# First loads of a transformer block: which queue issues them, in what order, and the last 64 weight rows by two transfers

## The chip, the cores and the metric

The kernel runs on one core of one Trainium2 chip. The metric is the device time of one execution in microseconds (us): the median of three runs is 211.99 us (211.5 to 212.01). A core has TensorE (PE in the profile; PEld is its weight loads), VectorE (DVE), ScalarE (ACT), GpSimd (POOL) and SyncE (SP). SP computes nothing here; its program is a list of DMA issues. ACT can issue DMAs too, between its own instructions. All DMAs of the core run on the same 16 DMA engines.

## The reference

```python
S, D, H, Dh, F, W = 2048, 448, 16, 28, 1792, 256
xn = layernorm(x)                                   # x: [1, 2048, 448], bf16
q, k, v = split(xn @ wqkv)                          # wqkv: [448, 3 * 448], 16 heads of 28
p = softmax(where(0 <= i - j < W, q k^T / sqrt(Dh), -1e9))
out = x + (p v) @ wo + (gelu(xn @ w_gate) * (xn @ w_up)) @ w_down
```

One layer normalisation feeds two branches that are added to x: attention in a sliding window of 256 keys, and a gated feed-forward layer.

## The kernel before

The 2048 rows of x are 16 tiles of 128 rows (tile t is `x_sb[:, t, :]`), in four blocks of 512 rows, numbered 0 to 3. For each block the kernel makes q and k transposed (`qT`, `kT`), four groups of four heads each, and v (`v_sb`), then scores, Exp on ACT, masks, the product with v, and the feed-forward layer; work of the next block, and the feed-forward products of this one, are woven in by lists (`plan`) that set the order by hand. Each engine runs its own list in order. A row that waits holds up all that is behind it on its engine.

The contraction length 448 is cut in 128 + 128 + 128 + 64 rows. The weight rows 0 to 383 are the dense part. The last 64 rows are held twice, on partitions 0 to 63 and 64 to 127, so that two products over 64 rows can run in the two halves of the PE array. Three tiles in SBUF take the weights of the first stage:

- `wraw` ([128, 4, 896]): the columns of q and k, raw. Its plane 3 takes the last 64 rows: q's columns on partitions 0 to 63, k's on 64 to 127.
- `wv` ([128, 4, 448]): the columns of v. Its plane 3 takes the last 64 rows of v twice.
- `wqp`, `wkp`, `w3p`: q's and k's weights with each head's 28 columns padded to 32. Engines copy them out of `wraw`: L754 a group or two of dense rows, L792 the last 64 rows for all groups (`w3p`).

The steps that the prediction follows, by line and in the order in which the program has them:

- L85 to L98: the first loads. x's tile 0 and tiles 2 and 3 are issued by SP, tile 1 by ACT (L87). ACT then issues the dense rows of q's and k's first 112 columns, that is of group 0 (L90). SP goes on with v's dense rows (L91), the last 64 rows in four transfers of 64 partitions (L93 twice, L95 twice), x's tiles 4 to 7 (L96), and the other 336 columns of q and of k (L98 twice), all on one queue.
- L152: nine products on zeroed data ahead of everything, and a tenth a little later.
- L157 to L200, for tiles 0 to 3: statistics (DVE), 1/sigma (ACT), normalisation (L176 on DVE, tile 1 L184 on ACT), four transposes on PE (L199), and a copy into `xnT` (L200).
- L204: v of tile 0 and then of tile 1, dense rows (`pv<-wv,xnT`), q and then k of group 0, dense rows (`s<-xnT,wqp` and `s<-xnT,wkp`).
- L210: the last 64 rows: q and k of group 0 with `w3p`, then v of tiles 0 to 3 with plane 3 of `wv`. L204 again: v of tile 3, and of tile 2 a little later.
- L257 and L258: the copies of q (ACT) and k (DVE) out of PSUM. L240: the copies of v. On DVE stand, right behind the first k copy, the L754 copies of group 1 (from the L98 loads), the copy of v's tile 3, the L754 copies of groups 2 and 3, and the copy of v's tile 2.
- L688 and L693: scores and Exp of group 0; L204 and L210: q and k of groups 1, 2 and 3.
- L505: the first feed-forward products (`ue<-xnT,wu`). They take a pair of the four PSUM banks b0 to b3, and the pair is free once q and k of group 2 have been copied out.

Every DMA that SP or ACT issues gets one of eight semaphores, DMAHW0 to DMAHW7, in turn. The transfer that takes a semaphore for the second time waits until the first one has landed. So SP can run at most eight transfers ahead, and a late one holds up the ninth behind it.

The few lines that a sentence can't say (before):

```python
    for c in (0, D):
        nc.scalar.dma_start(out=wraw[:, 0:3, c:c + 4 * Dh], in_=wqk[:, :, c:c + 4 * Dh])                 # L90
    nc.sync.dma_start(out=wv[:, 0:3, :], in_=rows(A_wqkv, 0, 3)[:, :, 2 * D:3 * D])                      # L91
    for a in range(2):
        nc.sync.dma_start(out=wraw[64 * a:64 * a + 64, 3, 0:D], in_=A_wqkv[384:448, a * D:(a + 1) * D])  # L93
...
    qk_halves(0, 0, pq, pk)                                  # PE: L210, needs w3p
    for t in range(4):
        v_half(t, pvs[t], t < 2)                             # PE: L210, needs wv[:, 3, :]
    qk_copies(0, 0, pq, pk)                                  # ACT L257, DVE L258
    pads(nc.vector.tensor_copy, wqp, slice(1, 2))            # DVE: L754, needs the L98 loads
    v_copy(0, pvs[0], nc.scalar.copy)
    v_copy(1, pvs[1], nc.scalar.copy)
    pads(nc.vector.tensor_copy, wkp, slice(1, 2))            # DVE: L754
    v_dense(3, pvs[3], False)
    v_copy(3, pvs[3], nc.vector.tensor_copy)                 # DVE: L240
```

Of the kernel before, what the change touches and what calls it, by code (L numbers as in the profile page):

```python
# [16 lines left out]
S, D, H, Dh, F = 2048, 448, 16, 28, 1792  # L17
# [10 lines left out]
def kernel(  # L28
# [11 lines left out]
    nc = tc.nc  # L40
# [23 lines left out]
    wv = const.tile([P, 4, D], bf16, name="wv")  # L64
    v_sb = const.tile([P, NT, H, 32], bf16, name="v_sb")
    wraw = blk.tile([P, 4, 2 * D], bf16, name="wraw", tag="hT")
# [5 lines left out]
    def rows(w, c0, n):  # L72
        return w[c0 * P:(c0 + n) * P, :].rearrange("(c p) n -> p c n", p=P)
# [10 lines left out]
    wqk = rows(A_wqkv, 0, 3)[:, :, 0:2 * D]  # L84
    nc.sync.dma_start(out=x_sb[:, 0, :], in_=xv[:, 0, :])  # L85
    nc.vector.memset(x_sb[:, 1, 0:1], 0.0)
    nc.scalar.dma_start(out=x_sb[:, 1, :], in_=xv[:, 1, :])  # L87
    nc.sync.dma_start(out=x_sb[:, 2:4, :], in_=xv[:, 2:4, :])
    for c in (0, D):
        nc.scalar.dma_start(out=wraw[:, 0:3, c:c + 4 * Dh], in_=wqk[:, :, c:c + 4 * Dh])  # L90
    nc.sync.dma_start(out=wv[:, 0:3, :], in_=rows(A_wqkv, 0, 3)[:, :, 2 * D:3 * D])  # L91
    for a in range(2):
        nc.sync.dma_start(out=wraw[64 * a:64 * a + 64, 3, 0:D], in_=A_wqkv[384:448, a * D:(a + 1) * D])  # L93
    for a in range(2):
        nc.sync.dma_start(out=wv[64 * a:64 * a + 64, 3, :], in_=A_wqkv[384:448, 2 * D:3 * D])  # L95
    nc.sync.dma_start(out=x_sb[:, 4:8, :], in_=xv[:, 4:8, :])  # L96
    for c in (0, D):
        nc.sync.dma_start(out=wraw[:, 0:3, c + 4 * Dh:c + D], in_=wqk[:, :, c + 4 * Dh:c + D])  # L98
    load_ffn(wu, B_w_up, slice(0, 3))
# [981 lines left out]
```

## Time and profile before

| what | value |
|---|---|
| time, median of three runs | 211.99 us (211.5 to 212.01) |
| span of the profiled execution, first to last instruction | 210.4 us |
| what the median has beyond the span (start and finish) | 1.6 us |
| PE busy | 205.3 us, 98% of the span |
| DVE, ACT, POOL busy | 156.6, 134.5, 44.3 us |
| DMA traffic | 15.68 MB in 24890 packets |

The profiled execution's own time is its span of 210.4 us and what lies around it; the times shown are those of the three runs. Starts in the profile are us from the first instruction. A row of the timeline has start, length, engine, line, operation, tile written <- tiles read, and how many instructions are merged in it; in brackets stands the idle time ahead of it and what ended it. PE's ends are modelled, so the starts of its rows are what to go by. SPq and ACTq rows are the issue of a DMA, not its transfer. A packet is one piece that one DMA engine moves, here a row of a tile.

### The profile page before, as it was taken

To read this page: it belongs to the slowest core of one execution; us is meant where nothing else is said; L and a number is where in the kernel's file an instruction comes from. 1 tells how busy PE (TensorE), PEld (TensorE's weight loads), DVE (VectorE), ACT (ScalarE), POOL (GpSimd) and SP (SyncE) were. 2 spreads that over 40 slices of the span, in tenths; PEclk is the share of its full clock that TensorE was granted. 3 is DMA by queue.
4 is the path that set the end of the run, shared out by engine and by line. 5 is a ranking of instruction groups with operands and counts; after the bars stand their busy time and mean duration, and the time that the engine had idled before them with its cause. 6 is when DMAs were issued, how large, how long until landed. Compare 5 with 4: busy or idle time off the path is not lost. (4 is left out here: it accounts for less than half of the span.)

```text
span 210.4 us, 6677 instructions
## 1 busy us (share of the span) xinstructions
PE 205.3 (98%) x2842; PEld 98.4 (47%) x2842; DVE 156.6 (74%) x360; ACT 134.5 (64%) x132; POOL 44.3 (21%) x89
## 2 busy tenths in 40 slices
PE   7899999999999999999999999999999999999994
PEld 2443444544454545444445444544444454544572
DVE  6798989899788985696438897395385699596532
ACT  4689896956677977413778788523587787756000
POOL 5289932241000220040000112013000022032000
PEclk9999999999999999999999999999999999999999
DMA  5999599973341001003331000100000010100011
GB/s 171 277 244 207 112 207 224 296 237 82 74 103 53 25 11 31 9 3 72 71 75 47 25 3 24 23 3 21 22 5 0 3 47 3 45 9 16 3 47 50
DMA packets 24890, 15.68 MB, mean 75 GB/s; under 512 B 9208, under 2 KB 24728, under 8 KB 24856
## 3 DMA queue, kind: packets, MB, share of 16 engines
q1 hardware_dynamic: 23912, 14.93, 30.2%
q8 instruction: 23, 0.38, 0.7%
q10 hardware_dynamic: 944, 0.29, 0.6%
q14 instruction: 11, 0.09, 0.2%
HBM read 9.26 MB, written 2.41 MB: 55 GB/s over the span
## 5 line engine op out<-in xcount | busy, mean ns | idle before, releaser
L693 ACT ACTIVATE p_sb<-sc 128x2048 bf16<-128x2048 f32 x38 | 71.4, 1879 | 16.9 <-PE sc L688 11.7
L545 ACT ACTIVATE p_sb<-gt 128x1024 bf16<-128x1024 f32 x28 | 28.6, 1025 | 31.3 <-PE gt L505 30.4
L628 POOL TENSOR_TENSOR oN<-oc,l 128x512 bf16<-128x512 f32 x16 | 20.7, 1298 | 120.5 <-DVE l L641 120.5
L505 PE MATMUL gt<-xnT,wg 64*128 64x512 bf16 x224 | 45.6, 376 | 0.0
L414 PE MATMUL po<-wd,hT 128*128 128x448 bf16 (+1 forms) x224 | 44.7, 347 | 0.0
L505 PE MATMUL gt<-xsw,wg 64*128 64x512 bf16 x168 | 40.7, 376 | 0.0
L613 DVE TENSOR_TENSOR p_sb<-p_sb,masks 128x256 bf16<-128x256 bf16 (+1 forms) x98 | 30.9, 369 | 7.4 <-ACT p_sb L693 7.4
L555 DVE TENSOR_TENSOR hT<-p_sb,u 128x512 bf16<-128x512 bf16 x34 | 21.8, 675 | 13.5 <-PE u L505 13.5
L414 PEld LDWEIGHTS <-hT 128*128 128x128 bf16 x238 | 21.9, 98 | 19.1 <-issue 2.2
L505 PEld LDWEIGHTS <-wg 64*128 64x128 bf16 x392 | 19.0, 94 | 22.3
L505 PEld LDWEIGHTS <-wu 64*128 64x128 bf16 x392 | 18.7, 94 | 22.2 <-issue 0.4
L505 PE MATMUL u<-xnT,wu 64*128 64x512 bf16 x136 | 28.1, 376 | 0.0
L505 PE MATMUL u<-xsw,wu 64*128 64x512 bf16 x102 | 24.7, 376 | 0.0
L505 PE MATMUL ue<-xnT,wu 64*128 64x512 bf16 x88 | 18.0, 377 | 0.0
L647 DVE TENSOR_TENSOR oc<-oc,ov 128x512 f32<-128x512 f32 (+1 forms) x16 | 10.4, 656 | 10.0 <-ACT oc L645 9.9
L505 PE MATMUL ue<-xsw,wu 64*128 64x512 bf16 x66 | 16.3, 377 | 0.0
L688 PE MATMUL sc<-qT,kT 28*64 28x320 bf16 (+4 forms) x736 | 16.2, 259 | 0.0
L402 DVE TENSOR_TENSOR res<-po,x_sb 128x448 bf16<-128x448 f32 (+1 forms) x14 | 8.1, 605 | 7.8 <-PE po L414 6.7
L688 PEld LDWEIGHTS <-kT 28*64 28x64 bf16 x736 | 8.1, 103 | 12.3 <-issue 11.0
L522 DVE CAST hT<-ue 128x512 bf16<-128x512 f32 x16 | 10.5, 685 | 2.7 <-PE ue L505 2.7
L645 ACT COPY oc<-ov 128x512 f32<-128x512 f32 x16 | 9.3, 585 | 4.0 <-PE ov L662 4.0
L641 DVE STREAM_TRANSPOSE l<-inv_all 128x512 f32<-128x512 f32 x16 | 11.1, 701 | 0.1
(115 smaller groups left out, 257.0 us busy)
## 6 DMA issues: line engine op xcount, KB each, us to landing
out_dram<-res SPq DMA_DIRECT2D x15, 112.0 KB
wd<-in_B_w_down_dram SPq DMA_DIRECT2D x2, 784.0 KB
x_sb<-in_A_x_dram SPq DMA_DIRECT2D x3, 448.0 KB
xsw<-xnT SPq DMA_DIRECT2D x6, 192.0 KB
wg<-in_B_w_gate_dram SPq DMA_DIRECT2D x2, 560.0 KB
wu<-in_B_w_up_dram SPq DMA_DIRECT2D x4, 224.0 KB
wu<-in_B_w_up_dram SPq DMA_DIRECT2D x2, 336.0 KB
wraw<-in_A_wqkv_dram SPq DMA_DIRECT2D x2, 252.0 KB
```

Source lines behind the costliest of these rows:

```text
L414: nc.tensor.matmul(po[:, 0:w], lhsT=x[:, k, tt * P:(tt + 1) * P], rhs=wt[:, k, lo:up], start=start and n == 0, stop=stop and n == len(term ...
L505: nc.tensor.matmul(ps, lhsT=w[64 * hi:64 * hi + 64, c, p * P:(p + 1) * P], rhs=xchunk(qb, hi, c, qb * QB, QB), start=c == 0, stop=c == 6, ...
L522: copy(out=hTs[qb][:, p + 7 * i, :], in_=us[i])
L545: nc.scalar.activation(out=ges[p][:, :, :], in_=gt[:, :, :], func=ACT.Gelu_apprx_tanh)
L555: nc.vector.tensor_tensor(out=hT[:, p + 7 * i, :], in0=ge[:, i, :], in1=u, op=ALU.mult)
L613: nc.vector.tensor_tensor(out=reg, in0=reg, in1=m, op=ALU.mult)
L628: nc.gpsimd.tensor_tensor(out=oN[:, g, :], in0=oc[:, :], in1=inv, op=ALU.mult)
L641: nc.vector.transpose(out=l1[:, :, :], in_=inv_all[:, 4 * qb + g, :].unsqueeze(2).to_broadcast([P, 16, 32]))
L645: nc.scalar.copy(out=oc[:, :], in_=ov[0][:, :])
L647: nc.vector.tensor_tensor(out=oc[:, q0:], in0=oc[:, q0:], in1=ov[1][:, q0:], op=ALU.add)
L688: nc.tensor.matmul(ss[k0:k0 + nk, j, col:col + nq], lhsT=kT[r, g, kt * P + k0:kt * P + k0 + nk], rhs=qT[r, g, ring(qb).start + q0:ring(qb) ...
L693: nc.scalar.activation(out=p_sb[:, :, 0:ncol], in_=ss[:, :, 0:ncol], func=ACT.Exp, scale=SCALE)
```

## The change

The first q and k columns move from ACT's queue to SP's, behind v's dense rows. x's tiles 4 to 7 move ahead of the last 64 rows. These rows come by two transfers in place of four: each writes all 128 partitions of plane 3 and reads a source of shape [2, 64, 448]. For q and k the source's first step goes from q's columns to k's; for v it has a step of zero, so the same 64 rows are read twice. Nothing else differs; lines behind the change have numbers smaller by two.

```diff
     nc.sync.dma_start(out=x_sb[:, 2:4, :], in_=xv[:, 2:4, :])
+    nc.sync.dma_start(out=wv[:, 0:3, :], in_=rows(A_wqkv, 0, 3)[:, :, 2 * D:3 * D])
     for c in (0, D):
-        nc.scalar.dma_start(out=wraw[:, 0:3, c:c + 4 * Dh], in_=wqk[:, :, c:c + 4 * Dh])
-    nc.sync.dma_start(out=wv[:, 0:3, :], in_=rows(A_wqkv, 0, 3)[:, :, 2 * D:3 * D])
-    for a in range(2):
-        nc.sync.dma_start(out=wraw[64 * a:64 * a + 64, 3, 0:D], in_=A_wqkv[384:448, a * D:(a + 1) * D])
-    for a in range(2):
-        nc.sync.dma_start(out=wv[64 * a:64 * a + 64, 3, :], in_=A_wqkv[384:448, 2 * D:3 * D])
+        nc.sync.dma_start(out=wraw[:, 0:3, c:c + 4 * Dh], in_=wqk[:, :, c:c + 4 * Dh])
     nc.sync.dma_start(out=x_sb[:, 4:8, :], in_=xv[:, 4:8, :])
+    nc.sync.dma_start(out=wraw[:, 3, 0:D], in_=A_wqkv[384:448, 0:2 * D].rearrange("p (a n) -> a p n", a=2))
+    nc.sync.dma_start(out=wv[:, 3, :], in_=A_wqkv[384:448, 2 * D:3 * D].unsqueeze(0).to_broadcast([2, 64, D]))
     for c in (0, D):
         nc.sync.dma_start(out=wraw[:, 0:3, c + 4 * Dh:c + D], in_=wqk[:, :, c + 4 * Dh:c + D])
```

SP's list from its first DMA, before; a row has the line, the tile written and the tensor read, the shape written, and the semaphores that the row waits for.

```order
L85 DMA x_sb<-in_A_x_dram 128x448
L88 DMA x_sb<-in_A_x_dram 128x2x448
L91 DMA wv<-in_A_wqkv_dram 128x3x448
L93 DMA wraw<-in_A_wqkv_dram 64x448 x2
L95 DMA wv<-in_A_wqkv_dram 64x448 [waits DMAHW0_49]
L95 DMA wv<-in_A_wqkv_dram 64x448 [waits DMAHW1_49]
L96 DMA x_sb<-in_A_x_dram 128x4x448 [waits DMAHW2_49]
L98 DMA wraw<-in_A_wqkv_dram 128x3x336 [waits DMAHW3_49]
L98 DMA wraw<-in_A_wqkv_dram 128x3x336 [waits DMAHW4_49]
```

The same stretch of SP's list with the change.

```order
L85 DMA x_sb<-in_A_x_dram 128x448
L88 DMA x_sb<-in_A_x_dram 128x2x448
L89 DMA wv<-in_A_wqkv_dram 128x3x448
L91 DMA wraw<-in_A_wqkv_dram 128x3x112 x2
L92 DMA x_sb<-in_A_x_dram 128x4x448
L93 DMA wraw<-in_A_wqkv_dram 128x1x448
L94 DMA wv<-in_A_wqkv_dram 128x1x448 [waits DMAHW0_49]
L96 DMA wraw<-in_A_wqkv_dram 128x3x336 [waits DMAHW1_49]
L96 DMA wraw<-in_A_wqkv_dram 128x3x336 [waits DMAHW2_49]
```

The last 64 rows (L93 and L95 before, L93 and L94 now) stand behind x's tiles 4 to 7 instead of ahead of them. The two loads of the other q and k columns waited for ACT's two q and k transfers (DMAHW3 and DMAHW4); now they wait for x's tiles 1 to 3 (DMAHW1 and DMAHW2).

ACT's list from its first DMA to the first normalisation, before.

```order
L87 DMA x_sb<-in_A_x_dram 128x448 [waits DVE_49]
L90 DMA wraw<-in_A_wqkv_dram 128x3x112 x2
L137 ACT_TABLE_LOAD
L166 ACTIVATE lnv<-mv_all,eps_t 128x1 [waits DVE_49]
L167 ACTIVATE rstd_all<-lnv 128x1 [waits Activation_49]
```

The same stretch with the change.

```order
L87 DMA x_sb<-in_A_x_dram 128x448 [waits DVE_49]
L135 ACT_TABLE_LOAD
L164 ACTIVATE lnv<-mv_all,eps_t 128x1 [waits DVE_49]
L165 ACTIVATE rstd_all<-lnv 128x1 [waits Activation_49]
L164 ACTIVATE lnv<-mv_all,eps_t 128x1 [waits DVE_49]
```

The two issues are gone from ACT; the rest of its list is as it was. The lists of PE, DVE and POOL hold the same rows in the same order.

## Prediction

> **What bounds the kernel now.** I read the page first, then the waits, then busy time by stage, then the timeline of the first 20 us engine by engine, last the DMA packets. Of the page, the span, PE's share, and PE and DMA over the span in 40 slices:
>
> ```profile
> span 210.4 us, 6677 instructions
> PE 205.3 (98%) x2842; PEld 98.4 (47%) x2842; DVE 156.6 (74%) x360; ACT 134.5 (64%) x132; POOL 44.3 (21%) x89
> ...
> PE   7899999999999999999999999999999999999994
> ...
> DMA  5999599973341001003331000100000010100011
> ```
>
> PE runs from end to end; DMA is full only in the first fifth. The waits of PE, over the whole span:
>
> ```profile
> PE wps L152 <- DVE wo L126: 1.4, 1, 1.4
> PE pv L204 <- DMA wv<-in_A_wqkv_dram: 0.6, 1, 0.6
> ```
>
> Only the second can be touched: 0.6 us for v's weights. Busy time by stage (PE, PEld, DVE, ACT, POOL, granted clock, DMA share, GB/s):
>
> ```profile
> 0.00:2.00 2.00, 0.57 (x2) 0.28 (x3) 0.99 (x8) 0.00 (x0) 1.32 (x7) 1.00 0.05 10
> 2.00:4.00 2.00, 2.00 (x7) 0.64 (x5) 1.06 (x4) 1.46 (x2) 1.66 (x2) 1.00 0.89 258
> ...
> 12.00:14.00 2.00, 2.00 (x25) 0.80 (x9) 2.00 (x5) 1.96 (x2) 1.73 (x7) 1.00 1.13 224
> 14.00:20.00 6.00, 6.00 (x79) 2.33 (x86) 5.81 (x15) 5.64 (x8) 5.45 (x18) 1.00 1.20 244
> 20.00:30.00 10.00, 10.00 (x222) 4.78 (x224) 8.35 (x18) 8.94 (x10) 7.67 (x27) 1.00 0.77 137
> ```
>
> From 12 to 20 us PE, DVE and ACT are all full, and so are the DMA engines. A delay that gets into the first 20 us has nowhere to be absorbed, and after that PE has no wait in which to catch up: it reaches the end. So the question is when the first loads land.
>
> The starts on PE:
>
> ```profile
> 7.34 0.73 PE L204 MATMUL pv<-wv,xnT 128*128 128x448 bf16 x3 [0.65 <-DMA wv<-in_A_wqkv_dram]
> ...
> 9.04 0.82 PE L204 MATMUL s<-xnT,wqp 128*128 128x512 bf16 x3
> ...
> 10.44 0.39 PE L210 MATMUL s<-xnT,w3p 64*128 64x512 bf16 x2
> 10.66 0.54 PE L210 MATMUL pv<-wv,xnT 64*128 64x448 bf16 x4
> ...
> 18.52 0.38 PE L505 MATMUL ue<-xnT,wu 64*128 64x512 bf16 x1
> ```
>
> And on DVE: a wait for x's tile 0, then what needs late weights:
>
> ```profile
> 2.94 0.63 DVE L157 BATCH_NORM_STATS2 st<-x_sb 128x6 f32<-128x448 bf16 x1 [0.91 <-DMA x_sb<-in_A_x_dram]
> ...
> 8.55 0.42 DVE L200 COPY xnT<-tp 128x512 bf16<-128x512 bf16 x1 [0.86 <-PE tp L199]
> ...
> 8.89 0.27 DVE L792 COPY w3p<-wraw 128x448 bf16<-128x448 bf16 x1
> ...
> 11.69 0.26 DVE L754 COPY wkp<-wraw 128x336 bf16<-128x336 bf16 x1
> ...
> 17.45 0.68 DVE L258 CAST kT<-pk 128x512 bf16<-128x512 f32 x1
> ```
>
> **The prices.** DMA queues (q1 is SP's, q10 ACT's) in three windows: packets, MB, share of 16 engines. First 4 to 8 us, then 8 to 10 us, then 81 to 86 us, this one with its share in 40 slices of 0.125 us:
>
> ```profile
> q1 hardware_dynamic: 1223, 1.00, 84.8%
> q10 hardware_dynamic: 591, 0.13, 15.1%
> ```
>
> ```profile
> q1 hardware_dynamic: 840, 0.56, 102.6%
> ```
>
> ```profile
> DMA  0016100101011212131222202212221210000000
> ...
> q1 hardware_dynamic: 144, 0.11, 13.9%
> k<-kT SPq DMA_DIRECT2D x4, 12.0 KB
> k<-qT SPq DMA_DIRECT2D x3, 16.0 KB
> ```
>
> A row of 896 B: 0.848 x 16 x 4 us / 1223 = 44 ns on its engine. A row of 224 B: 0.151 x 64 us / 591 = 16 ns. A row of 672 B (most of the second window): 1.026 x 32 us / 840 = 39 ns. The third window holds seven transfers whose outermost dimension is 4, in flight together. They are given 0.139 x 80 = 11.1 us of engine time within slices 9 to 33, that is 3.1 us: 3.6 engines at work on average, where the 128-row loads of the first microseconds keep all 16 busy. A transfer with an outermost 4 seems to run on four engines.
>
> **The change, part by part.** *v's rows ahead of the q and k columns.* In front of v's rows now stand only x's tiles 0 to 3; the two column loads (768 rows of 224 B, 48 per engine, 0.8 us) no longer share the engines with them. They land up to 0.8 us earlier, and the wait of 0.65 us at 7.34 goes. Next late is the copy of tile 3's transposes (8.55), which moves with PE; q of group 0 starts near 8.5 instead of 9.04: 0.5 us ahead. The q and k columns are behind v now, but by the same count they end no later than before.
>
> *ACT without its two issues, SP with them.* DVE's first statistics and ACT's first use of them, then SP's waits:
>
> ```profile
> 3.60 0.18 DVE L158 BATCH_NORM_AGGREGATE mv_all<-st 128x2 f32<-128x6 f32 x1
> ...
> 3.82 0.29 ACT L166 ACTIVATE lnv<-mv_all,eps_t 128x1 f32<-128x1 f32 x1
> ```
>
> ```profile
> SPq L98 <- DMA wraw<-in_A_wqkv_dram: 1.7, 2, 1.3
> ```
>
> For ACT it is nothing: its first work waits for DVE's statistics, which end at 3.8. SP gets two issues and drops two. x's tiles 4 to 7 and the loads behind them go out earlier, since fewer issues stand ahead of them and L98 no longer waits 1.7 us for ACT's transfers. PE had no other wait for a load, so this is worth nothing to it, but it keeps the DMA queues full.
>
> *The last 64 rows in two transfers.* This is the term that decides. Each writes 128 partitions from a source whose outermost dimension is 2. No transfer of before pairs 128 with 2. One bound is all 16 engines, 8 rows each, 0.35 us a transfer. The other, going on from the outermost 4 above, is two engines, 64 rows each, 64 x 44 = 2.8 us. I take two engines: the row with the outermost 4 is the nearest, and a split over the outermost dimension that both sides share allows no more.
>
> [...]
>
> When do they land? An engine has in front of them 88 rows of x and v (11 x 128 rows over 16 engines) and 48 short rows: 88 x 44 + 48 x 16 ns = 4.7 us. It starts at 1.9 (5% of the first 2 us). So on the two engines q's and k's rows move from 6.6 to 9.4 and v's to 12.2, and only then their share of the other q and k columns (24 rows of 39 ns a load, 0.94 us each): 13.1 and 14.1. What lands is seen later than counted: tile 0 counts 1.9 + 8 x 0.044 = 2.25 and DVE starts at 2.94, 0.7 later. With 0 to 0.7 us added, k's columns are usable between 14.1 and 14.8; I take 14.5, and for v's rows 12.6.
>
> PE stands before v's last rows at 10.1 (10.66 less the 0.5 gained) and waits until 12.6: 1.9 us behind before. DVE stands before the L754 copy of k's columns, at 11.69 before, and goes on at 14.5: 2.8 us behind, with v's copies, two statistics, four normalisations and the k copies queued behind it. DVE makes up 0.2 (idle in 14 to 20 us). The k copy of group 2 frees the PSUM banks for the first `ue` products; it ends at 18.13 and they start at 18.52, a margin of 0.4. So `ue` starts 2.8 - 0.2 - 0.4 = 2.2 us late, and PE's own 1.9 is inside that. `w3p`, about 1.2 us late, is hidden behind the wait for v's rows.
>
> **The sum.** The gain of 0.5 is swallowed by the later wait; +2.2 us remain. On the span: 210.4 + 2.2 = 212.6. The median lies 1.6 above the span and the change doesn't touch what lies there, so 211.99 + 2.2 = 214.2. This case reaches from 213.2 (rows of 41 ns and no lag: k's columns at 13.5, 1.8 - 0.6 = 1.2 us) to 215.3. That end comes from v's dense rows before: 1.9 + 56 x 0.044 + 0.8 = 5.2 counted, 7.34 seen; if 1.5 of these 2.1 us come on top of 14.1, DVE goes on at 15.6, 3.9 - 0.6 = 3.3 us late.
>
> **Rivals.** *Spread over all engines.* If the two transfers use 16 engines, each takes 0.35 us, they land at about 7.3 plus the lag, ahead of PE's need at 9.9, and what stays is the gain: 0.5 us, 211.5. For it: the written side has 128 partitions, as the fast loads have. Against it: the outermost-4 rows. It decides if both have landed by 10.1, that is if a transfer takes less than (10.1 - 6.6 - 0.7) / 2 = 1.4 us. [...]
>
> *Two engines, but the delay is covered.* Rows of 35 ns and no lag put k's columns at 13.0: 1.3 - 0.6 = 0.7 us, and about 0.1 less if DVE uses what it has free in 20 to 30 us (8.35 of 10): 212.6. Against it: 44 ns is the mean of a full queue, and these two engines stay full.
>
> *The backlog reaches the next block.* Two engines carry 2 x 56 extra rows, 4.9 us, and a transfer has landed only when its slowest engine is done; everything until 20 us is full, and 20 to 30 us has 2.3 us free. The swap of the next block's rows and its first use:
>
> ```profile
> 22.79 2.31 SPq L486 DMA_DIRECT2D xsw<-xnT  x2
> ```
>
> ```profile
> 29.78 0.73 PE L339 MATMUL pv<-wvs,xsw 64*128 64x448 bf16 x6
> ```
>
> From the end of the issue to the use are 4.7 us, and PE is 2.2 late itself; if landing takes over 2 us there, the swap is what PE waits for, and the shift is between 2.6 and 4.9: about 3.5, 215.5.
>
> **Chances.** Two engines with a stall of about 2.2 us: 0.60. Spread, with the gain: 0.20. Backlog in the next block: 0.12. Covered: 0.08. What a measurement can tell from no change is about 0.3%, 0.64 us. The spread case (-0.5) is mostly inside it: 0.13 same, 0.07 faster; the covered case is 0.05 same, 0.03 slower. So faster 0.07, same 0.18, slower 0.75. The likeliest case alone has 213.2 to 215.3; with the spread case and part of the backlog the range is 211.4 to 215.3.
>
> **What would show it.** Right: the wait of PE for `wv` at 7.3 gone, and in its place a wait of about 2 us before the L210 products with `wv` (start near 12.6 in place of 10.66); DVE waiting at L754 for `wraw` until about 14.5; `ue` starting near 20.7; the DMA share low between the end of the other engines' work and these landings. Wrong: L210 for v starts by 10.3, then the rows were spread; or `ue` starts within 0.6 us of 18.52, then the banks did not tie PE to DVE; or PE waits again near 30, then the backlog was not worked off.

## The result and the profile after

| | median us | range, executions | span of the profiled execution |
|---|---|---|---|
| before | 211.82 | 211.5 to 212.01, 4 | 210.4 us |
| with the change | 217.41 | 216.48 to 218.63, 4 | 214.8 us |

The ratio is 1.0267, with a 95% interval of 1.024 to 1.0294: slower by 5.6 us. The forecast had the sign, but 2.2 us, and its range ended at 215.3. The profiled execution, at 216.48 us, is the fastest of its four.

The page of the changed kernel: span, PE's busy time, then PE, the granted clock and the DMA engines in 40 slices of 5.4 us.

```profile
span 214.8 us, 6669 instructions
...
PE 206.7 (96%) x2837; PEld 98.9 (46%) x2842; DVE 156.3 (73%) x360; ACT 134.6 (63%) x132; POOL 43.6 (20%) x89
...
PE   7859999999999999999999999999999999999994
...
PEclk9978999999999999999999999999999999999999
DMA  6799959993443000100541000100100010100011
```

What PE's row loses is in the third slice, 10.7 to 16.1 us; after it PE is as full as before, though busy doesn't mean fast. The clock row has a 7 and an 8 in the third and fourth slice, where there is a stretch of lower clock now: TensorE was slowed there.

PE's waits over the whole span, the costliest and the one that goes with the last 64 rows of q and k (the name `masks` is a memset that DVE runs right behind the `w3p` copy):

```profile
PE pv L208 <- DMA wv<-in_A_wqkv_dram: 2.4, 1, 2.4
...
PE s L208 <- DVE masks L791: 0.5, 1, 0.5
```

PE's timeline, start and length first:

```profile
6.75 0.88 PE L202 MATMUL pv<-wv,xnT 128*128 128x448 bf16 x3
...
8.59 0.82 PE L202 MATMUL s<-xnT,wqp 128*128 128x512 bf16 x3
...
10.60 0.39 PE L208 MATMUL s<-xnT,w3p 64*128 64x512 bf16 x2 [0.55 <-DVE masks L791]
13.43 0.56 PE L208 MATMUL pv<-wv,xnT 64*128 64x448 bf16 x4 [2.44 <-DMA wv<-in_A_wqkv_dram]
13.93 1.30 PE L202 MATMUL pv<-wv,xnT 128*128 128x448 bf16 x3
...
15.74 1.30 PE L202 MATMUL pv<-wv,xnT 128*128 128x448 bf16 x3
...
22.83 0.38 PE L503 MATMUL ue<-xnT,wu 64*128 64x512 bf16 x1
```

The wait for `wv` at 7.3 is gone and q starts at 8.59 in place of 9.04, as forecast. Then PE waits until 13.43 for v's last rows. The three products behind it take 1.30 us, where three of the same shape took 0.73 at 7.34 in the kernel before. `ue` starts at 22.83 in place of 18.52, 4.31 late (forecast 2.2). PE's products for the next block, seen by their group:

```profile
34.09 0.73 PE L337 MATMUL pv<-wvs,xsw 64*128 64x448 bf16 x6
```

They started at 29.78 before: 4.31 late as well. So all of the loss of this execution is there by `ue`, and none is added or won back behind it.

DVE's timeline:

```profile
10.27 0.28 DVE L790 COPY w3p<-wraw 128x448 bf16<-128x448 bf16 x1 [1.74 <-DMA wraw<-in_A_wqkv_dram]
...
14.65 0.32 DVE L752 COPY wqp<-wraw 128x336 bf16<-128x336 bf16 x1 [2.04 <-DMA wraw<-in_A_wqkv_dram]
15.72 0.28 DVE L752 COPY wkp<-wraw 128x336 bf16<-128x336 bf16 x1 [0.75 <-DMA wraw<-in_A_wqkv_dram]
...
21.63 0.69 DVE L256 CAST kT<-pk 128x512 bf16<-128x512 f32 x1 [0.28 <-PE pk L208]
```

The `wkp` copy starts at 15.72; before it was 11.69, forecast was 14.5. In the last row, the k copy of group 2 that frees the banks, DVE waits for PE: here PE, not DVE, is the later one.

Busy time by stage (PE, PEld, DVE, ACT, POOL, granted clock, DMA share, GB/s):

```profile
13.00:14.00 1.00, 0.57 (x5) 0.19 (x5) 0.00 (x0) 0.18 (x1) 0.86 (x4) 0.93 1.09 205
14.00:17.00 3.00, 3.00 (x23) 0.97 (x24) 1.60 (x5) 1.85 (x3) 2.16 (x9) 0.50 1.03 213
17.00:18.00 1.00, 0.95 (x5) 0.38 (x4) 1.00 (x3) 0.81 (x1) 0.12 (x1) 0.86 0.80 184
```

The granted clock falls to 0.50. What is missing to 1.00 is 0.07 + 3 x 0.50 + 0.14 = 1.71 us, that is half speed for 3.4 us, from 13.86 to 17.27. Nothing in the forecast had that.

The DMA engines from 6 to 10 us, in 40 slices of 0.1 us:

```profile
DMA  9999987653333311111195946689999643577668
```

In slices 15 to 20, 7.4 to 8.0 us, the share is 1 in 10: about two engines of 16 at work while the rest have nothing. In the window from 7.5 to 8 us SP's queue has 27 packets and 14.1% of the 16 engines' time, 42 ns a packet: the two engines are no slower there than the 44 ns of the forecast. Then the loads behind come into the queue and the other engines go on with those.

### The profile page after: what moved, and what is told of

It reads as the page before. It is cut to its first block, busy times and chain, and to the rows that moved or that the text cites. A ratio compares the mean times of both kernels' runs of the same rounds, so it can differ in the third digit from the quotient of the medians.

```text
span 214.8 us, 6669 instructions
## 1 busy us (share of the span) xinstructions
PE 206.7 (96%) x2837; PEld 98.9 (46%) x2842; DVE 156.3 (73%) x360; ACT 134.6 (63%) x132; POOL 43.6 (20%) x89
## 5 line engine op out<-in xcount | busy, mean ns | idle before, releaser
L553 DVE TENSOR_TENSOR hT<-p_sb,u 128x512 bf16<-128x512 bf16 x34 | 21.8, 676 | 13.5 <-PE u L503 13.5
```

Of the source, the lines that this page charges most:

```text
L553: nc.vector.tensor_tensor(out=hT[:, p + 7 * i, :], in0=ge[:, i, :], in1=u, op=ALU.mult)
```

## The experiments

My theory after the result had three parts: the two transfers run on two engines; DVE's late columns give most of the loss; and PE, left empty for 2.4 us, is slowed, which gives the rest. The rivals: the new order or the move of the issues from ACT to SP does it; or only one of PE and DVE matters. Times and ratios, each with the kernel before on the same chip; "clock" is the mean granted clock of each execution:

| kernel | median us (range, executions) | before | ratio, 95% | clock |
|---|---|---|---|---|
| `four` | 211.75 (211.37 to 211.82, 10) | 211.74 | 0.9999, 0.9989 to 1.0008 | 1.00 |
| `two` | 218.52 (217.87 to 218.71, 4) | 211.55 | 1.031, 1.0282 to 1.0338 | 0.992, 0.984 x3 |
| `col_late` | 214.3 (214.12 to 214.82, 4) | 211.55 | 1.0126, 1.0099 to 1.0153 | 1.00 |
| `v_two` | 213.95 (213.43 to 214.44, 4) | 211.55 | 1.0103, 1.0072 to 1.0134 | 1.00 |
| `qk_two` | 214.92 (214.07 to 216.0, 4) | 211.55 | 1.0166, 1.0117 to 1.0214 | 1.00 x2, 0.992 x2 |
| `fill` | 216.09 (215.58 to 216.6, 4) | 211.74 | 1.0209, 1.0184 to 1.0233 | 1.00 |
| `fill5` | 216.24 (215.91 to 216.76, 4) | 211.6 | 1.0211, 1.0197 to 1.0226 | 1.00 |
| `late` | 217.15 (216.9 to 217.93, 4) | 211.74 | 1.0268, 1.0243 to 1.0292 | 0.992 x3, 0.984 |
| `late_fill` | 215.6 (215.17 to 216.32, 4) | 211.74 | 1.0176, 1.0159 to 1.0193 | 1.00 |
| `after_again` | 216.77 (216.51 to 218.38, 6) | 211.6 | 1.026, 1.0234 to 1.0285 | 0.992 x5, 0.984 |
| `probe` | 212.45 (1) | 211.53 | | 0.996 |

### Which part of the change loses: `four` and `two`

`four` is the changed kernel with the last rows by four transfers again, at the new place:

```diff
-    nc.sync.dma_start(out=wraw[:, 3, 0:D], in_=A_wqkv[384:448, 0:2 * D].rearrange("p (a n) -> a p n", a=2))
-    nc.sync.dma_start(out=wv[:, 3, :], in_=A_wqkv[384:448, 2 * D:3 * D].unsqueeze(0).to_broadcast([2, 64, D]))
+    for a in range(2):
+        nc.sync.dma_start(out=wraw[64 * a:64 * a + 64, 3, 0:D], in_=A_wqkv[384:448, a * D:(a + 1) * D])
+    for a in range(2):
+        nc.sync.dma_start(out=wv[64 * a:64 * a + 64, 3, :], in_=A_wqkv[384:448, 2 * D:3 * D])
```

> The change, but the last 64 rows come by the four 64-partition transfers of before, at the new place. Theory (each of the two transfers ran on two engines): all engines share the rows, they land near 8.5, PE does not wait at L210 and what stays is the gain from v's earlier rows: -0.5 us, about 211.3. Rival (order and queues of the change are at fault, not the two transfers): as slow as the change, 216 to 218.

Its PE timeline:

```profile
9.99 0.54 PE L210 MATMUL pv<-wv,xnT 64*128 64x448 bf16 x4
...
17.84 0.38 PE L505 MATMUL ue<-xnT,wu 64*128 64x512 bf16 x1
```

No wait, and a time equal to before within 0.1%: the whole loss is the two transfers, and order and queue are worth nothing either way. The gain of 0.5 us that was expected did not come. `ue` at 17.84 is 0.7 earlier than in the trace of before, but the wait of 0.65 us that was to be won isn't in every execution: with the same loads of v's dense rows as before, `late` has no wait at 7 us, `col_late` 0.20 and `late_fill` 0.59. The profiled execution of before, at 211.99 us, lies at the upper end of its four.

`two` is the other side: the kernel before with only its four transfers replaced by the two.

> Before, with nothing changed but the last 64 rows: the two transfers of the change in the place of the four. Theory (the two transfers alone make the loss, by running on two engines): the same 128 rows of backlog on two engines, now ahead of x's tiles 4 to 7, so DVE's statistics of tile 4 and the other q and k columns wait too: k's columns at DVE near 15.5, a slow PE after the wait, 216 to 218. Rival (the loss needs the new order, with x's tiles ahead of the rows): under 213.5.

It is the slowest of all, +7.0 us, and above the 216 to 218 expected: k's columns reach DVE at 17.26, not near 15.5. The two slow transfers stand ahead of x's tiles 4 to 7 here, so these come late too. Its DVE, then its PE:

```profile
14.63 0.63 DVE L155 BATCH_NORM_STATS2 st<-x_sb 128x6 f32<-128x448 bf16 x1 [4.77 <-DMA x_sb<-in_A_x_dram]
...
17.26 0.28 DVE L752 COPY wkp<-wraw 128x336 bf16<-128x336 bf16 x1 [0.29 <-DMA wraw<-in_A_wqkv_dram]
```

```profile
12.26 0.56 PE L208 MATMUL pv<-wv,xnT 64*128 64x448 bf16 x4 [1.96 <-DMA wv<-in_A_wqkv_dram]
...
16.84 0.66 PE L686 MATMUL sc<-qT,kT 28*64 28x320 bf16 x16 [3.19 <-DVE kT L256]
```

DVE waits 4.77 us for x's statistics, which stand ahead of the first k copy, and PE waits 3.19 us for that copy. So of the change's parts, moving x's tiles ahead of the slow rows spared some of their cost.

### How many engines: `probe`

The kernel before, with six small transfers in a quiet stretch. Each writes the same scratch tile, so SP issues one only when the one before has landed:

```diff
+        if qb == 2:
+            last64 = A_wqkv[384:448, 2 * D:2 * D + 224]
+            for n in (1, 16, 8, 4, 2, 1):
+                src = xv[:, 0, 0:224] if n == 1 else last64[0:P // n].unsqueeze(0).to_broadcast([n, P // n, 224])
+                nc.sync.dma_start(out=probe[:, :], in_=src)
```

> The kernel before, with six small transfers added in a quiet stretch of the DMA engines, behind the swap of the last block's rows; each writes the same scratch tile of 128 partitions with 448 B on each, so each waits until the one before it has landed, and the steps between their issues are the times from issue to landing. The first and the last read 128 plain rows; between them the sources have an outermost dimension of 16, 8, 4 and 2, with a step of zero. Theory (as many engines as the outermost dimension, rows of about 30 ns, between 16 ns for 224 B and 39 ns for 672 B): 16 lands like the plain one, 8 takes 0.2 us more, 4 takes 0.7 us more, 2 takes 1.7 us more; during the 2 the DMA share is near 0.13. Rival (the late landings in the changed kernel come from the backlog at the start, or from the reading of the same rows twice, not from the outermost dimension): all six steps are within 0.3 us of each other, or grow with the number of copies instead.

SP's own timeline, the issues for n = 16, 8, 4, 2 and the last plain one:

```profile
109.57 0.61 SPq L897 DMA_DIRECT2D probe<-in_A_wqkv_dram  x1
...
112.99 0.68 SPq L897 DMA_DIRECT2D probe<-in_A_wqkv_dram  x1
...
115.43 0.57 SPq L897 DMA_DIRECT2D probe<-in_A_wqkv_dram  x1
...
118.06 0.53 SPq L897 DMA_DIRECT2D probe<-in_A_wqkv_dram  x1
...
121.46 0.35 SPq L897 DMA_DIRECT2D probe<-in_A_x_dram  x1
```

The packets of SP's queue between these issues, in the same order, and for n = 2 the DMA share in slices of 0.085 us:

```profile
q1 hardware_dynamic: 144, 0.06, 6.6%
q8 instruction: 1, 0.02, 1.8%
...
q1 hardware_dynamic: 136, 0.06, 9.2%
...
q1 hardware_dynamic: 132, 0.06, 7.9%
...
DMA  0000060000000000000111111111111111000000
...
q1 hardware_dynamic: 130, 0.06, 6.0%
```

Each transfer has 128 rows and some packets more: 16, 8, 4 and 2, the number of the outermost dimension. For n = 2 the share stands at 1 in 10 in 15 slices, 1.3 us, flat: two engines (the 6 ahead of them is another packet of q8). The largest share in a slice is 5 tenths for n = 8 and 3 for n = 4, that is about 8 and 5 of 16. So I read the packets beyond the rows as one for each engine; for n = 16, where the packet of q8 fills the largest slice, the count stands alone. The steps are 3.42 us (n = 16), 2.44, 2.63 and 3.40 (n = 2). From 4 to 2 it is 0.77 us more for 32 more rows of 448 B on each engine, 24 ns a row. The expectation had 1.0 there, and 0.5 from 8 to 4 where 0.19 was measured. Against a plain transfer nothing can be said: behind the last one no issue waits for its landing, and the first, 2.67 us to the next issue, starts among other loads (65.7% of the 16 engines in that window). The step for n = 16 was to be the shortest of the four and is the longest; what happened there is in the last section. The rival, that it is the backlog or the double read, falls: the number of copies goes down from 8 to 2 while the steps grow by 0.96 us, and these windows hold next to nothing but the transfer itself.

### DVE's columns alone: `col_late`

The kernel before with only the two loads of the other q and k columns (L98) moved behind the first two loads of `wu`.

```diff
-    for c in (0, D):
-        nc.sync.dma_start(out=wraw[:, 0:3, c + 4 * Dh:c + D], in_=wqk[:, :, c + 4 * Dh:c + D])
     load_ffn(wu, B_w_up, slice(0, 3))
+    for c in (0, D):
+        nc.sync.dma_start(out=wraw[:, 0:3, c + 4 * Dh:c + D], in_=wqk[:, :, c + 4 * Dh:c + D])
```

> Before, with the loads of the other q and k columns (L98, on all engines) moved behind the first two wu loads. v's last rows and w3p are on time, only DVE's L754 copies wait, until about 14.1 in place of 11.69. Theory (ue starts later by DVE's lateness less 0.6): 2.4 - 0.6 = 1.8 us, 213.6, and no slow clock, since PE's wait stays near 1 us. Rival (DVE's wait is not on the path, PE's wait for v's rows made the loss): within 0.6 us of before.

Its DVE and its PE:

```profile
14.49 0.32 DVE L754 COPY wkp<-wraw 128x336 bf16<-128x336 bf16 x1 [0.70 <-DMA wraw<-in_A_wqkv_dram]
```

```profile
20.00 0.38 PE L505 MATMUL ue<-xnT,wu 64*128 64x512 bf16 x1
20.80 0.39 PE L505 MATMUL ue<-xsw,wu 64*128 64x512 bf16 x2 [0.42 <-DVE kT L258]
```

The second of these rows in the kernel before:

```profile
18.53 0.59 PE L505 MATMUL ue<-xsw,wu 64*128 64x512 bf16 x2
```

By chance the `wkp` copy starts at the forecast's 14.5. `ue` waits for the k copy, and its second row stands at 20.80, where before it stood at 18.53: 2.27 late for 2.80 on DVE. The forecast's own step, lateness less 0.6, gives 2.2. So DVE's chain through the PSUM banks is real, at full clock and with v's rows on time. The median is 2.7 us above before, for 1.8 expected with the columns at 14.1; 0.5 of the 2.7 is the wait at 7 us, 0.65 in the profiled execution of before and 0.20 in this one.

### One of the two transfers: `v_two` and `qk_two`

The changed kernel with q's and k's last rows by two 64-partition transfers again (`v_two`), or with v's (`qk_two`).

> The change, but only v's last rows by the new transfer (zero step); q's and k's rows by two 64-partition transfers. Half the rows are left on two engines: v's rows land near 10.5, when PE wants them, k's columns near 12.8 in place of 11.69. Theory (two loads in a row on two engines; DVE's lateness less 0.6 us is what reaches ue; no slow clock without a long wait): 1.1 - 0.6 = 0.5 us, 212.2. Rival (each of the two transfers has its price, half of the loss): +2.8, 214.5.

> The change, but only q's and k's last rows by the new transfer; v's rows by two 64-partition transfers. w3p's rows land near 10.2, k's columns near 12.8. Theory: as with v's rows alone, 0.5 us from DVE, and up to 0.5 more since PE wants w3p at 9.8: 212.2 to 212.7. Rival (half of the loss each): 214.5.

Both cost much more than a stall of one transfer was taken to cost: +2.4 and +3.4 us. The theory's 212.2 is missed in both, and the rival's 214.5 is nearer: that each transfer has a price of its own isn't excluded. PE of `v_two`, then of `qk_two`:

```profile
11.59 0.56 PE L209 MATMUL pv<-wv,xnT 64*128 64x448 bf16 x4 [1.31 <-DMA wv<-in_A_wqkv_dram]
```

```profile
11.83 0.39 PE L209 MATMUL s<-xnT,w3p 64*128 64x512 bf16 x2 [1.99 <-DVE masks L792]
```

Their `wkp` copies start at 14.18 and 14.55, 2.5 and 2.9 late, though each drops 64 of the 128 rows of 896 B on the two engines. Why they are so late I did not test. It isn't a packet of instructions as in `probe` (last section): q8 has none in either trace from 0 to 16 us.

### The clock: `fill`, `fill5`, `late`, `late_fill`, `after_again`

`fill` is the changed kernel with 11 products on zeroed data ahead of the products with v's last rows. They write a half of a PSUM tile that nothing reads. (They read `warm`, which is a part of the tile `wo`; the trace has 10 of the 11.)

```diff
     qk_halves(0, 0, pq, pk)
+    for _ in range(11):
+        nc.tensor.matmul(s0[1][:, 1, :], lhsT=warm[:, 0:P], rhs=warm[:, 0:QB], start=True, stop=True)
```

> The change, with eleven products on zeroed data (128x512, 0.216 us each, into a free PSUM bank) behind the q and k products with w3p, so that PE works in most of its wait of 2.4 us. Theory clock (PE came out of the wait at half speed, and that cost 1.5 us of the 4.3): the v products after the wait take 0.74 us for three in place of 1.30, ue starts 2.8 us later than before, not 4.3, and the time is about 214.6. Rival DVE (the columns for DVE land at 15.7, and DVE alone holds ue at 4.0 - 0.2 - 0.4 = 3.4 us): 215.2 at best. If the speed has no part in it: 217.4.

Its PE, and its DVE:

```profile
10.93 2.55 PE L801 MATMUL s<-wo 128*128 128x512 bf16 x10
13.41 0.55 PE L208 MATMUL pv<-wv,xnT 64*128 64x448 bf16 x4
13.90 0.74 PE L202 MATMUL pv<-wv,xnT 128*128 128x448 bf16 x3
...
22.30 0.39 PE L503 MATMUL ue<-xsw,wu 64*128 64x512 bf16 x2 [0.41 <-DVE kT L256]
```

```profile
16.03 0.28 DVE L752 COPY wkp<-wraw 128x336 bf16<-128x336 bf16 x1 [1.23 <-DMA wraw<-in_A_wqkv_dram]
```

v's products start at 13.41 as in the changed kernel, but the three behind them take 0.74, full speed. PE is now early and waits 0.41 for DVE's k copy. The first k copy, which reads the other half of the tile, waits 1.48 us for the zero products here, but the `wkp` copy behind it waits for its load all the same. So with the clock kept up, DVE alone holds the loss at +4.4 us by the medians: both figures for DVE and clock, 215.2 and 214.6, were too low. The clock was worth 1.3 us against 217.41, or 0.7 against the later 216.77: what DVE's lateness covers of it doesn't show.

`late` turns it round: the kernel before with v's last rows (two transfers, 16 engines) moved behind the first two loads of `wu`, so that PE waits and DVE's columns are on time. `late_fill` is `late` with 14 zero products.

> Before, with v's last rows (the two transfers of L95, 64 partitions each, spread over all engines) moved behind the first two wu loads. They land near 14.1 in place of 8, so PE waits about 3.4 us at L210, while w3p and DVE's columns are on time. Theory clock: 3.4 + 1.5 = 4.9 us, 216.7, and the products behind the wait take 1.30 us for three. Rival (a wait costs only its length): +3.4 us, 215.2.

> The same with fourteen products on zeroed data in the wait (3.0 us). Both theories: +3.4 us, 215.2, no slow products. What it lacks against the kernel without the fourteen products is the price of the slow clock: 1.5 us by the theory clock, 0 by the rival.

PE of `late`, then of `late_fill`:

```profile
13.71 0.81 PE L210 MATMUL pv<-wv,xnT 64*128 64x448 bf16 x4 [3.49 <-DMA wv<-in_A_wqkv_dram]
...
15.70 1.30 PE L204 MATMUL pv<-wv,xnT 128*128 128x448 bf16 x3
```

```profile
14.74 0.73 PE L210 MATMUL pv<-wv,xnT 64*128 64x448 bf16 x4 [0.88 <-DMA wv<-in_A_wqkv_dram]
15.40 0.74 PE L204 MATMUL pv<-wv,xnT 128*128 128x448 bf16 x3
```

In the profiled execution of `late_fill` v's rows came 1.0 us later than in that of `late`, and still the kernel is faster by 1.55 us in the median. So where PE was the later one, keeping it busy was worth 1.55 us. (The zero products hold DVE up too: its k copy waits 3.33 us for them. But the next copy of v then waits 1.24 for PE, so DVE isn't the one that is waited for.)

`fill5` has 5 zero products in place of 11: the empty wait becomes shorter and doesn't vanish.

> The changed kernel with only 5 zero products (128x512, 0.21 us each) in PE's wait in place of 11; they write a PSUM half that nothing reads, ahead of the L208 products with v's last rows. The wait of 2.4 us becomes one of about 1.3. Theory (what slows the clock is the length of the empty wait: no execution is slowed behind the 1.3 us wait of v_two, some behind the 2.0 us wait of qk_two, all behind the 2.4 us of the changed kernel): mean clock 1.00 in every execution and the time of fill, 216.1 (+4.4). Rival (any wait of over 1 us in this stretch slows the clock): mean clock 0.992, granted clock 0.5 for some 3.4 us behind the v products, 216.5 or more, as the changed kernel. Both: ue starts at 22.3 or later, since DVE's k columns come no earlier.

```profile
14.13 0.55 PE L208 MATMUL pv<-wv,xnT 64*128 64x448 bf16 x4 [0.96 <-DMA wv<-in_A_wqkv_dram]
14.61 0.74 PE L202 MATMUL pv<-wv,xnT 128*128 128x448 bf16 x3
```

Behind this wait of 0.96 us the three products take 0.74 us, and the mean granted clock is 0.998, in the other three executions 0.999 or 1.0. The time is that of `fill`: the theory's number, though not for its reason: the length of a wait alone doesn't tell (last section). Ahead of the fill, this execution has another wait, 1.80 us for `w3p`, with no slow stretch behind it either.

> The changed kernel itself once more, for more executions of it. Theory (the clock is halved for whole stretches of 3.4 us, one or two of them by execution): each execution has a mean granted clock of 0.992 (one stretch, 1.7 us lost of 215) or 0.984 (two), and the times lie in two groups, 216.4 to 216.9 and 218.0 to 218.7, with nothing between. Rival (the scatter comes from the landing of the loads): one mean clock in all of them, and times spread evenly from 216.4 to 218.7.

With the first four there are ten executions of the changed kernel. Seven have a mean clock of 0.992 (median 216.76 us), three have 0.984 (218.0, 218.38, 218.63). A mean of 0.992 is (1 - 0.992) x 215 / 0.5 = 3.4 us at half speed, 0.984 is 6.9: one stretch or two. The second costs 1.6 us. One execution with 0.992 took 217.51 and stands between the groups, so the landing of the loads may scatter too (the `wkp` copy starts at 15.72 in the first trace and at 16.10 in that of `after_again`), and "nothing between" was too strict. `qk_two` shows the same step: 214.07 and 214.20 without a slow stretch, 215.64 and 216.0 with one. Its profiled execution, with a wait of 1.99 us, is one of the two without; how long PE waited in the other two isn't on record.

## Why the prediction was wrong

**Right.** *The wait for v's weights* at 7.3 is gone and q starts 0.45 us earlier. *ACT's issues* are worth nothing (`four`, together with the new order). *Two engines* for an outermost 2: `probe` shows it by count (130 packets for 128 rows) and by a share of 1 in 10; and `four`, which has the halves as transfers of their own, is 5.6 us faster than the changed kernel. *DVE's chain* to `ue` by the lateness less 0.6: `col_late` has 2.27 for 2.80. *No backlog* in the next block: 4.31 late at 22.83 and at 34.09. The rivals *spread* and *covered* fall with 13.43 and 22.83.

**The step that failed: "DVE goes on at 14.5: 2.8 us behind".** It went on at 15.72 in the first trace, 16.10 in `after_again`, 16.03 and 16.78 in `fill` and `fill5`. Counted and seen, by the rows above: q's and k's rows 9.4 and 10.27, v's 12.2 and 13.43, q's columns 13.1 and 14.65, k's 14.1 and 15.72. So 0.87 of the 1.62 us was there at the first of the four. Two terms of the sum were too small, by the packet records of the first trace. One is the way from the last packet to the engine that waits: v's last row ends at 12.45 and the last of k's columns at 14.90, and they are seen 0.98 and 0.82 us later, where I had allowed 0 to 0.7. The other is the price of the late rows: k's columns end 0.80 later than counted. The rows of 896 B on the two engines took 43 ns from 8 to 11.5 us, as counted, but the last 27 of them 59, and the rows of 672 B behind them 58 in place of 39. The prediction had a row that warned of this, v's dense rows seen 2.1 us later than counted, and put it only at the end of the range. The mean of the four starts is 16.16, 4.5 us late; less 0.6 that is 3.9. (The lower end of the range, too, is a little off: rows of 41 ns from the same start at 6.6 put k's columns at 13.7, not 13.5. Nothing here hangs on it.)

**A false base.** Lateness was counted from the trace of before, which had a wait at 7 us that other executions don't have. Against an execution without it DVE is some 0.5 us later still (its `wkp` copy starts at 11.42 in `probe`, whose first loads are those of before, and at 11.08 in `late`): 3.9 + 0.5 = 4.4, near what `fill` and `fill5` measure over before (4.35 and 4.64). For the same reason the gain of 0.5 isn't in the medians (`four`).

**A term that was missing: "PE's own 1.9 is inside that".** PE's wait, 2.44 us, was indeed shorter than DVE's delay. But the granted clock was 0.50 behind it for 3.4 us, or for 6.9 by the mean clock of 0.984. With one such stretch PE comes level with DVE's lateness and goes past it, 216.76 less 216.1 to 216.2: +0.6; with two, +2.2. Why the clock falls behind some waits and not behind others the runs do not show (last section).

**The sum as measured.** DVE's late columns 4.4, the clock 0.6 or 2.2: 216.8 or 218.4 from 211.75; ten executions have 216.76 and 218.38 as the middle of their groups. The clock's 0.6 and 2.2 are taken from these groups, so this sum is no test of them; for the clock's share stand `fill` and `late_fill`.

**What stays open.** Why rows became dearer from 11.5 us on: it isn't the two engines alone, for the rows of 768 B that the others move took 40 ns from 11.5 to 12 us and 61 to 68 from 12 to 13.5. Why `v_two` and `qk_two` cost 2.4 and 3.4 us where 0.5 to 1.0 were counted. And what sets off a stretch of half clock. One transfer with the 64 rows outermost, the two halves inside, was not tried.

## What to carry to other kernels

Before merging two DMAs into one, look at the outermost dimension of both sides: here [2, 64, 448] put 128 rows on two engines and cost 5.6 us, where four transfers of 64 rows cost nothing. A load that came late was paid twice here: by DVE, which waited longest (+4.4 us in `fill`, at full clock), and by TensorE at a granted clock of 0.50 for 3.4 us behind a wait of 2.44 (1.55 us in `late` against `late_fill`). So price the waits of every engine that the load feeds, and look at the granted clock behind PE's. And measure a wait that is to be won in more than one execution before it is counted as a gain.

## What the runs showed that was not expected

- **Stretches of half clock.** By the mean granted clock of the stages, 1.71 us of full speed are missing in the changed kernel's first trace, 1.72 in `after_again` (0.58 from 13.4 to 17.5 us) and 1.69 in `late` (0.71 from 13.4 to 17.5, 0.80 from there to 20): 3.4 us at 0.50 in each. `two` has more, by stage:

```profile
14.00:20.00 6.00, 2.95 (x22) 1.24 (x24) 4.93 (x13) 3.72 (x6) 3.06 (x12) 0.50 0.77 179
```

  Six microseconds at 0.50 without a break, and by its mean clock of 0.984 some 6.9 us in all.

- **The length of a wait alone doesn't tell what the clock does.** A wait of 1.99 us left the clock full (`qk_two`), one of 1.96 was followed by half speed (`two`). PE's longest waits for a load or for DVE from 9 to 15 us, and the mean granted clock in a stretch behind them:

| run | waits, us | stretch, us | granted clock |
|---|---|---|---|
| `late` | 3.49 | 13.4 to 17.5 | 0.71 |
| changed kernel | 0.55, 2.44 | 14 to 17 | 0.50 |
| `after_again` | 0.86, 2.40 | 13.4 to 17.5 | 0.58 |
| `two` | 1.96 | 13 to 14 | 0.61 |
| `qk_two` | 1.99, 0.60 | 10.9 to 17.5 | 1.00 |
| `fill5` | 1.80, 0.96 | whole span | 0.998 |
| `col_late` | 1.48, 0.20 | 13.4 to 17.5 | 1.00 |
| `v_two` | 1.31 | 10.9 to 17.5 | 1.00 |
| `late_fill` | 0.88 | 13.4 to 17.5 | 1.00 |

What decides between 1.96 and 1.99 us these runs do not show; and of the executions that were not profiled only the mean clock is known.

- **A packet of instructions in the slowest step.** In `probe` the step for n = 16 was 3.42 us, longer than for 8 and 4. In that window stands one packet of the queue q8, instructions, 0.02 MB with 1.8% of 16 engines' 3.42 us: 0.98 us on one engine. By narrower windows it starts near 110.96, so it ends near 111.94. Of the 128 rows none starts from 111.62 to 111.90; eight follow from 111.90 to 112.26, and SP issues the next transfer at 112.99. My reading of these times is that the eight stood behind the instructions' packet on one engine and that SP waited for them: some 0.65 us of the step.
- **Packets beyond the rows.** For 128 rows `probe` has 144, 136, 132 and 130 packets with an outermost 16, 8, 4 and 2. That is how the engines were counted here, in a quiet window.
